# The seam between two expert layers: more PSUM banks and another order of products, and four of eight sums of x^T made earlier and kept in DRAM

## The chip, the core and the metric

One core of one Trainium2 chip runs the whole program. The metric is the device time of one execution in microseconds. The engines are named as in the profile: PE (TensorE's matrix products; PEld is its weight loads), DVE (VectorE), ACT (ScalarE), POOL (GpSimd) and SP (the queue that issues the DMAs).

## What is computed

A windowed attention feeds a first expert layer with a rational activation, and its result feeds a second one with an ELU activation. All data are float32.

```python
x = attention(q, k, v)              # 2304 tokens, 512 features
h = x @ w_in                        # layer 1: 512 -> 2048
P = a[0] + a[1]*h + a[2]*h**2 + a[3]*h**3
Q = 1.0 + abs(b[0])*abs(h) + abs(b[1])*h**2
x = (P / (Q + 1e-6)) @ w_out        # 2048 -> 512
h = x @ w2_in                       # layer 2: 512 -> 2048
g = where(h > 0, h, exp(min(h, 0)) - 1)
out = g @ w2_out                    # 2048 -> 512
```

## The kernel before, in words

Activations lie transposed, features on the partitions (`xT`). Every float32 operand of a product is split into a high part (rounded to fp32r by ACT) and a low part (the rest, a subtraction on DVE, line L864 in layer 2); a product is three passes on PE: high*high, low*high, high*low.

**Layer 1** goes over six blocks of 384 tokens and, in each, over 16 chunks of 128 hidden features: 96 steps `s`, with `f = s % 16`. In step `s` PE makes `gemm1(s)` (L251, 12 matmuls) and then `gemm2_T(s-3)` (L699, 12 matmuls), which takes the activation of three chunks earlier. `rational(s)` makes the activation. Its instructions stand in this order on the engines, and each engine works them off in that order. ACT: square L279, abs L280, two affine ones L281 and L284, then a logarithm L298 that needs DVE's `qq` of the same step, an exponential L299, and then what `after()` adds. DVE: L292 (high part of the chunk before), L295 (`qq` of this chunk), a slot `beside[1]`, L304, a slot `beside[2]`, L309, L312, L313. POOL makes the low part (L310).

**The last pass** (s = 80 to 95, the last block) also prepares layer 2. Layer 2 does its first product by a scheme with seven half-size products instead of eight (named b11, b21, t2, t3, t1, t4, b22), for which it needs four sums of x^T (two halves each: eight sums, L885, numbers n = 0 to 3) and four sums of the weights (`sum_w`, L837). The list `AT_ACT` says which high parts ACT copies at the end of which step, by `f`; the list `AT_DVE` holds the sums and the low parts, two of which the function `next_one` takes out per step, into the two slots of `rational`, from `f >= 3` on. A low part reads its high part.

**The seam** is the change from layer 1 to layer 2. Three `gemm2_T` (chunks 93 to 95, called G0, G1, G2 of pair 0) are left and are put between the products of pair 0. From there on layer 2 goes over pairs `q` of hidden chunks. Each pair has seven products (L907), added up on DVE from PSUM (L963: h11, u, v, h22, u2, h21, h12), four ELUs (ACT L969, L973, high part L995; DVE L978, low part L864), and four second products G0 to G3 (L923) of the pair before. The operands of pairs 1 and 2 (A to F) are prepared beside them. PE's order is written out by hand in `second(q)`; the order of the other engines comes from a planner, `in_order`, with estimated costs and due times. Two things in it are numbers: the time at which it takes ACT and DVE to be free.

PSUM has eight banks. At the seam banks 0 to 3 hold the accumulators of `gemm2_T`; 4, 5 and 7 the last three `h`; 6 the `qa` of `rational`. `m_first` says which bank each of the first seven products takes, after that banks 6 and 7 alternate. A product waits until the bank's last reader is done: the product b21 of pair 0, in bank 4, for L313 of step 94.

Of the kernel before, what the change touches and what calls it, by code (L numbers as in the profile page):

```python
# [44 lines left out]
def kernel(  # L45
# [13 lines left out]
    nc = tc.nc  # L59
# [627 lines left out]
    def experts():  # L687
# [182 lines left out]
        def sum_x(J, n, eng=nc.gpsimd, ks=range(2)):  # L870
# [9 lines left out]
            for k in ks:  # L880
# [3 lines left out]
                )[n]  # L884
                eng.tensor_tensor(out=sums[J, n][k], in0=x, in1=y, op=ALU.subtract)  # L885

        def hi_op(J, nm, k):
            if nm[0] == "t":
                src = sums[J, int(nm[1]) - 1][k]
            else:  # L890
                src = x_row(J, k + 2 * (nm[1] == "2"), nm[2] == "2")
            s = "_".join(map(str, x_slots[2 * ORDER.index(nm) + k]))
            XO[J, nm, k] = t = wpool.tile([P, 2, TB], F32R, tag=s, name=f"xo_{s}")
            nc.scalar.activation(out=t[:, 0], in_=src, func=AF.Copy)
            low_part[J, nm, k] = (t[:, 1], src, t[:, 0])

        m_banks = cycle((6, 7))
        m_first = [7, 4, 6, 7, 4, 6, 7]

        def product(q, nm):  # L900
            x, side = LIES[FACTOR[nm]]
# [110 lines left out]
        def second_product(q, n):  # L1012

            if q == 0:
                if n < 3:
                    step((q, "G", n), "PE", 2080, lambda: gemm2_T(NCH - 3 + n))
                return
            nm = ("h11", "h22", "h21", "h12")[n]
            x = "EF"[int(nm[1]) - 1]
            T = int(nm[2]) - 1  # L1020
            before = [((q - 1) // NP2 * NP2, "out", T, t) for t in range(NTT)]
            step((q, "G", n), "PE", 2080, lambda: gemm2(q - 1, nm), (q - 1, "lo", nm), (q - 1, "lo", x), *before)
# [52 lines left out]

        def second(q):
            p = q % NP2
            multiply(q, "b11", (q - 1, "h21"))
            multiply(q, "b21", (q - 1, "h12"))
            second_product(q, 0)  # L1080
            multiply(q, "t2", (q, "m1"))
            multiply(q, "t3", (q, "h11"))
            second_product(q, 1)
            multiply(q, "t1", (q, "u"))
            second_product(q, 2)
            multiply(q, "t4", (q, "v"))
            multiply(q, "b22", (q, "h22"), (q, "u2"))
            second_product(q, 3)
            step((q, "m1"), "ACT", 390, copy_of(q, "b11", "qq0"), (q, "b11"), (q - 1, "rest", "h22"))
            step((q, "h11"), "DVE", 480, added(q, "h11", "m1", "b21", "qq1"), (q, "m1"), (q, "b21"), (q - 1, "rest", "h11"))  # L1090
            elu_steps(q, "h11", "h11", "h2", [(q - 1, "lo", "h21")], [(q - 1, "G", 0)])
            step((q, "u"), "DVE", 480, added(q, "u", "m1", "t2", "ee0"), (q, "m1"), (q, "t2"), (q - 1, "rest", "h12"))
            step((q, "v"), "DVE", 480, added(q, "v", "u", "t3", "ee1"), (q, "u"), (q, "t3"), (q - 1, "rest", "h21"))
            step((q, "h22"), "DVE", 480, added(q, "h22", "v", "t1", "qq0"), (q, "v"), (q, "t1"))
            step((q, "u2"), "DVE", 480, added(q, "u", "u", "t1"), (q, "v"), (q, "t1"))
            elu_steps(q, "h22", "h22", "oo", [(q - 1, "lo", "h12")], [(q, "G", 1)])
            step((q, "h21"), "DVE", 480, added(q, "v", "v", "t4"), (q, "h22"), (q, "t4"))
            elu_steps(q, "h21", "v", "h2", [(q, "lo", "h11")], [(q - 1, "G", 2)])
            step((q, "h12"), "DVE", 480, added(q, "u", "u", "b22"), (q, "u2"), (q, "b22"))
            elu_steps(q, "h12", "u", "oo", [(q, "lo", "h22")], [(q - 1, "G", 3)])  # L1100
            weight_steps(q)
            if q == 0:
                x_steps(0, ("t4", "b22"), -1)
            if q > 0 and p == 0:
                for T in range(2):
                    for t in range(NTT):
                        step((q, "out", T, t), "ACT", 500, lambda T=T, t=t: put_out(q, T, t, "A"), (q, "G", 2 + T),
                             *[(q + 2 - 3, nm) for nm in ("b11", "b21", "t4", "t3", "b22")])
            if p == NP2 - 1 and q + 1 < NQ:
                x_sums(q // NP2 + 1, q)  # L1110
                x_steps(q // NP2 + 1, ORDER, q)

        def in_order():

            users, due, at_pe = {}, {}, 0
            for key, (_, _, _, needs) in todo.items():
                for n in needs:
                    users.setdefault(n, []).append(key)
            ideal = {}
            for key in pe_order:  # L1120
                ideal[key] = at_pe
                at_pe += todo[key][1]

            def begin(key):
                if key not in due:
                    engine, cost = todo[key][:2]
                    lag = cost + (3500 if engine == "SP" else 250)
                    t = min([begin(u) for u in users.get(key, [])], default=at_pe) - lag
                    due[key] = min(t, ideal.get(key, t))
                return due[key]  # L1130

            for key in todo:
                begin(key)
            free = {"PE": 0, "ACT": 3400, "DVE": 5500, "POOL": 0, "SP": 0}
            done, left, order, np = {}, dict(todo), [], 0
            missing = {key: sum(n in todo for n in set(needs)) for key, (_, _, _, needs) in todo.items()}
            ready = {key: 0 for key in todo if not missing[key]}
            while left:
                best = None
                for engine in free:  # L1140
                    cand = [(max(t, free[engine]), due[k], k) for k, t in ready.items() if todo[k][0] == engine]
                    if engine == "PE":
                        cand = [c for c in cand if c[2] == pe_order[np]]
                    if cand:
                        t0 = min(c[0] for c in cand)
                        c = min((c for c in cand if c[0] <= t0 + 60), key=lambda c: c[1])
                        if best is None or c[0] < best[0]:
                            best = c
                t, _, key = best
                engine, cost, fn, _ = todo[key]  # L1150
                free[engine] = t + cost
                end = t + cost + (3500 if engine == "SP" else 200)
                order.append((t, len(order), fn))
                del left[key], ready[key]
                np += engine == "PE"
                done[key] = end
                for u in users.get(key, []):
                    missing[u] -= 1
                    if not missing[u]:
                        ready[u] = max(done[n] for n in todo[u][3] if n in done)  # L1160
            return [fn for _, _, fn in sorted(order, key=lambda o: o[:2])]
# [10 lines left out]
        def x_hi(n, *ks):  # L1172
            return [lambda k=k: hi_op(0, ORDER[n], k) for k in ks]

        def w_hi(names):
            return [lambda x=x: hi_w(0, x) for x in names]

        AT_ACT = {6: x_hi(0, 0, 1), 9: w_hi("AB"), 10: x_hi(1, 0, 1), 11: w_hi("C") + x_hi(2, 0),
                  12: x_hi(2, 1) + w_hi("D"), 13: x_hi(3, 0, 1), 14: x_hi(4, 0, 1)}
        AT_DVE = [lambda n=n, k=k: sum_x(0, n, nc.vector, (k,)) for n in range(4) for k in range(2)]  # L1180
        AT_DVE += [lambda: lo((0, ORDER[0], 0)), lambda: lo((0, ORDER[0], 1))]
        AT_DVE += [lambda n=n: sum_w(0, nc.vector, (n,)) for n in range(4)]
        AT_DVE += [lambda key=key: lo(key) for key in (
            (0, "A"), (0, "B"), (0, ORDER[1], 0), (0, ORDER[1], 1), (0, "C"), (0, ORDER[2], 0),
            (0, ORDER[2], 1), (0, "D"), (0, ORDER[3], 0), (0, ORDER[3], 1), (0, ORDER[4], 0), (0, ORDER[4], 1),
        )]

        def prepare(s):
            f = s - LAST
            if f == 3:  # L1190
                load_wi(0)
            if f == 14:
                load_wi(1)
                for e in raw_ones(0):
                    load_raw(0, e)

            def copies():
                for fn in AT_ACT.get(f, []):
                    fn()

            def next_one():
                if f >= 3 and AT_DVE:
                    AT_DVE.pop(0)()
            rational(s, beside=(lambda: None, next_one, next_one), after=copies)

# [3 lines left out]

        SK = 3  # L1210
        nj = 0
        for s in range(NCH):
            o = s - SK
            j, f = divmod(s, KF)
# [10 lines left out]
                nj += 1  # L1225
            elif s >= LAST:
                prepare(s)
            else:
                rational(s, beside=(go_on, go_on, go_on))
            if s == KF - 2:  # L1230
# [45 lines left out]
```

## Time and profile before

| | |
|---|---|
| time, median of 3 runs | 932.92 us (931.76 to 934.11) |
| the profiled execution's own time | 933.09 us |
| its span, first to last instruction | 931.4 us |
| PE busy | 913.8 us, 98% |
| DVE busy | 792.0 us, 85% |
| ACT busy | 741.9 us, 80% |

Attention takes the first 150 us or so, the six passes of layer 1 go on to 540 us, layer 2 from there to the end. A profile's time column is counted from the first instruction. A row of the timeline gives the start, the duration, the engine, the line, what is written from what, and in brackets how long the engine had been idle before it and what released it. Durations reach to the acknowledged write; the next instruction on the same engine can start some 0.09 us before that.

### The profile page before, as it was taken

How to read it: one execution, taken by the hardware profiler on the slowest of the kernel's cores; microseconds unless marked ns; L12 is line 12 of the kernel's file. 1: busy time of each engine (PE TensorE's matmuls, PEld its weight loads, DVE VectorE, ACT ScalarE, POOL GpSimd, SP SyncE). 2: the span in 40 equal slices, each digit the busy share in tenths (PEclk: the TensorE clock that was granted, in tenths of full speed). 3: DMA queues.
4: the chain of work that ended last, by engine and by line, in shares of the span. 5: the costliest groups of instructions: out<-in, count | busy, mean ns of one | idle time of the engine just before them, and what ended most of it. 6: DMA issues, size and time to landing. Idle time of an engine off the chain costs nothing.

```text
span 931.4 us, 16710 instructions
## 1 busy us (share of the span) xinstructions
PE 913.8 (98%) x5494; PEld 838.8 (90%) x5494; DVE 792.0 (85%) x1863; ACT 741.9 (80%) x1623; POOL 185.2 (20%) x260
## 2 busy tenths in 40 slices
PE   8999999999999999999999989999999999999998
PEld 5777778999999999999999988898989898888887
DVE  7899998998998998988989999998968688677653
ACT  6999999889898898889888987666876567767553
POOL 5566661122222222222222210000000000000000
PEclk9999999999999999999999999999999999999999
DMA  9899951012222212222200133445243323442201
GB/s 195 217 242 230 236 154 67 1 35 68 86 68 79 89 56 92 85 63 86 86 30 29 38 110 113 158 157 171 91 162 110 115 81 100 147 147 80 80 0 68
DMA packets 112423, 98.35 MB, mean 106 GB/s; under 512 B 62800, under 2 KB 86096, under 8 KB 112336
## 3 DMA queue, kind: packets, MB, share of 16 engines
q1 hardware_dynamic: 109936, 96.70, 35.2%
q10 hardware_dynamic: 2400, 0.59, 0.4%
q8 instruction: 43, 0.70, 0.3%
q14 instruction: 44, 0.36, 0.1%
HBM read 79.96 MB, written 17.30 MB: 104 GB/s over the span
## 4 chain that ended last, share of the span: by engine, by line
PE 79%; DVE 14%; ACT 3%; DMA 2%; issue 1%; DVEq 0%; ACTq 0%; SPq 0%
PE acc L923 21%; PE m L907 18%; PE acc L699 18%; PE h L251 18%; DVE pr_wi L494 2%; DVE pr_wo L494 1%; DVE cvt L146 1%; PE s_ps L468 1%; DVE qkT L437 1%; DVE ghi L292 1%; PE x L561 1%; DVE ee L313 1%; DMA q_wo<-in_q_dram 1%; PE ps_pT L542 1%; DVE w_wi L160 1%
## 5 line engine op out<-in xcount | busy, mean ns | idle before, releaser
L251 PE MATMUL h<-xs,w_wi 128*128 128x384 f32 x1152 | 216.9, 335 | 0.0
L251 PEld LDWEIGHTS h<-xs,w_wi 128*128 128x128 f32 x1152 | 200.7, 188 | 1.2 <-DVE xs L227 0.6
L699 PE MATMUL acc<-ghi,w_wo 128*128 128x384 f32 x768 | 194.8, 334 | 0.0
L310 POOL TENSOR_TENSOR glo<-ee,rr 128x384 fp32r<-128x384 f32 x92 | 93.7, 1018 | 312.4 <-DVE ee L309 109.3
L699 PEld LDWEIGHTS acc<-ghi,w_wo 128*128 128x128 f32 x768 | 138.6, 188 | 0.0
L699 PE MATMUL acc<-glo,w_wo 128*128 128x384 f32 x384 | 128.4, 334 | 0.5 <-DVE glo L310 0.5
L923 PE MATMUL acc<-op_wo,ghi 128*128 128x512 f32 x288 | 90.0, 393 | 0.0
L907 PE MATMUL m<-xo_wo,op_wi 128*128 128x384 f32 x336 | 77.0, 337 | 2.3 <-DVE ee L963 2.3
L907 PE MATMUL m<-xo_wi,op_wi 128*128 128x384 f32 x336 | 78.0, 340 | 0.0
L969 ACT ACTIVATE oo<-qq 128x384 f32<-128x384 f32 x24 | 12.6, 526 | 77.0 <-DVE qq L963 77.0
L699 PEld LDWEIGHTS acc<-glo,w_wo 128*128 128x128 f32 x384 | 72.1, 188 | 0.8 <-DVE glo L310 0.8
L298 ACT ACTIVATE rr<-qq,c_q 128x384 f32<-128x384 f32 x96 | 59.2, 617 | 16.5 <-DVE qq L295 15.7
L281 ACT ACTIVATE oo<-h,a_sb 128x384 f32<-128x384 f32 x96 | 68.0, 708 | 3.3 <-DVE h L312 3.2
L284 ACT ACTIVATE ee<-h,a_sb 128x384 f32<-128x384 f32 x96 | 67.7, 705 | 0.0
L907 PEld LDWEIGHTS m<-xo_wo,op_wi 128*128 128x128 f32 x336 | 61.3, 189 | 6.4 <-ACT oo L973 2.5
L295 DVE SCALAR_TENSOR_TENSOR qq<-h,b_abs,qa 128x384 f32<-128x384 f32 x92 | 56.1, 610 | 12.4 <-ACT qa L280 11.3
L292 DVE TENSOR_TENSOR ghi<-ee,rr 128x384 fp32r<-128x384 f32 x96 | 53.5, 558 | 12.2 <-ACT h L279 0.5
L313 DVE TENSOR_TENSOR ee<-ee,h 128x384 f32<-128x384 f32 x96 | 53.3, 555 | 10.4 <-DVE h L312 0.5
L923 PEld LDWEIGHTS acc<-op_wo,ghi 128*128 128x128 f32 x288 | 53.8, 189 | 9.0
L907 PEld LDWEIGHTS m<-xo_wi,op_wi 128*128 128x128 f32 x336 | 61.1, 189 | 0.0
L279 ACT ACTIVATE h<-h 128x384 f32<-128x384 f32 x96 | 46.3, 483 | 14.8 <-PE h L251 14.2
L963 DVE TENSOR_TENSOR ee<-ee,m 128x384 f32<-128x384 f32 x96 | 52.8, 551 | 5.8 <-PE m L907 5.5
(192 smaller groups left out, 2068.4 us busy)
## 6 DMA issues: line engine op xcount, KB each, us to landing
pair<-joined_wo SPq DMA_DIRECT2D x43, 256.0 KB, 2.6
raw_wo<-in_moe_w_out_dram SPq DMA_DIRECT2D x20, 512.0 KB, 4.7
raw_wi<-in_moe_w_in_dram SPq DMA_DIRECT2D x16, 512.0 KB, 4.3
half<-in_moe_w_in_dram SPq DMA_DIRECT2D x32, 256.0 KB, 2.7
two_wo<-joined_wi SPq DMA_DIRECT2D x32, 256.0 KB, 2.8
s<-sums SPq DMA_DIRECT2D x32, 256.0 KB, 2.9
half<-in_moe_w_out_dram SPq DMA_DIRECT2D x22, 256.0 KB, 2.8
v<-in_v_dram SPq DMA_DIRECT2D x32, 128.0 KB, 3.3
```

What stands on the lines that cost most here:

```text
L251: nc.tensor.matmul(h, lhsT=WT["wi", f][:, SEL[wp], kk * P:(kk + 1) * P], rhs=x[xp][kk], start=(kk == 0 and n == 0), stop=(kk == KD - 1 and ...
L281: nc.scalar.activation(out=oo, in_=h2, func=AF.Identity, scale=a_sb[:, 3:4], bias=a_sb[:, 1:2])
L284: nc.scalar.activation(out=ee, in_=h2, func=AF.Identity, scale=a_sb[:, 2:3], bias=a_sb[:, 0:1])
L292: nc.vector.tensor_tensor(out=hi, in0=ee0, in1=rr0, op=ALU.mult)
L295: nc.vector.scalar_tensor_tensor(out=qq, in0=h2, scalar=b_abs[:, 1:2], in1=qa, op0=ALU.mult, op1=ALU.add)
L298: nc.scalar.activation(out=rr, in_=qq, func=AF.Ln, bias=c_q)
L310: (nc.gpsimd if c > 4 else nc.vector).tensor_tensor(out=low, in0=ee0, in1=rr0, op=ALU.mult)
L313: nc.vector.tensor_tensor(out=ee, in0=ee, in1=h, op=ALU.add)
L699: nc.tensor.matmul(acc_t[d], lhsT=WT["wo", f][:, SEL[wp], d * P:(d + 1) * P], rhs=gt[SEL[xp]], start=(f == 0 and n == 0), stop=(f == KF - ...
L907: nc.tensor.matmul(out, lhsT=w[:, SEL[wp], c0:c0 + P], rhs=XO[q // NP2, nm, k][:, SEL[xp]], start=(k == 0 and n == 0), stop=(k == 1 and n ...
L923: nc.tensor.matmul(acc_t[T, t], lhsT=gt[SEL[xp]][:, t * P:(t + 1) * P], rhs=w[:, SEL[wp]], start=(first and n == 0), stop=(last and n == 2),)
L963: nc.vector.tensor_tensor(out=t, in0=R[q, x], in1=M[q, m], op=ALU.add)
```

## The change

Three things are changed together.

1. Of the eight sums of x^T, the four with n = 0 and n = 2 are made in the middle passes, in steps 40, 48, 56 and 64, in which no other work takes the slots. Each is written to DRAM at once, and `load_sum` reads them back in steps 83 and 84. The four that are left are taken out from `f >= 4` on, and the two low parts of the product t4 stand at the end of the list; ACT's copies for t4 are added at f = 15.
2. The products of pair 0 take other banks, stand in another order among G0, G1 and G2, and wait for other things.
3. The planner takes ACT and DVE to be free 1200 and 1500 ns later.

```diff
+        EARLY = ((0, 0), (0, 1), (2, 0), (2, 1))
+        def store_sum(i):
+            n, k = EARLY[i]
+            b11, b12, b22 = [x_row(0, k + 2 * r, T) for r, T in ((0, 0), (0, 1), (1, 1))]
+            x, y = (b12, b11) if n == 0 else (b22, b12)
+            t = row("ghi3" if nj % 2 else "glo3")
+            nc.vector.tensor_tensor(out=t, in0=x, in1=y, op=ALU.subtract)
...
+            nc.sync.dma_start(out=stored[n][:, k * TB:(k + 1) * TB], in_=t)
+        def load_sum(n):
...
+            nc.sync.dma_start(out=t.rearrange("p k c -> p (k c)"), in_=stored[n])
-        m_first = [7, 4, 6, 7, 4, 6, 7]
+        m_first = [7, 4, 6, 5, 7, 4, 5]
...
-            multiply(q, "b11", (q - 1, "h21"))
-            multiply(q, "b21", (q - 1, "h12"))
+            multiply(q, "b11", (q - 1, "u" if q == 1 else "h21"))
+            multiply(q, "b21", *[(q - 1, n) for n in (("h22", "u2") if q == 1 else ("h12",))])
...
+            before = {"t2": "m1", "t3": "h11", "t1": "u", "t4": "v", "b22": "h22 u2"}
+            if q == 0:
+                before = {"t2": "", "t3": "", "t1": "m1", "t4": "h11", "b22": "v"}
...
-                x_steps(0, ("t4", "b22"), -1)
+                x_steps(0, ("b22",), -1)
...
-            free = {"PE": 0, "ACT": 3400, "DVE": 5500, "POOL": 0, "SP": 0}
+            free = {"PE": 0, "ACT": 4600, "DVE": 7000, "POOL": 0, "SP": 0}
...
-                  12: x_hi(2, 1) + w_hi("D"), 13: x_hi(3, 0, 1), 14: x_hi(4, 0, 1)}
-        AT_DVE = [lambda n=n, k=k: sum_x(0, n, nc.vector, (k,)) for n in range(4) for k in range(2)]
+                  12: x_hi(2, 1) + w_hi("D"), 13: x_hi(3, 0, 1), 14: x_hi(4, 0, 1), 15: x_hi(5, 0, 1)}
+        AT_DVE = [lambda n=n, k=k: sum_x(0, n, nc.vector, (k,)) for n in (1, 3) for k in range(2)]
...
+            (0, ORDER[5], 0), (0, ORDER[5], 1),
...
-                if f >= 3 and AT_DVE:
+                if f >= 4 and AT_DVE:
...
+        STORE_AT = [j * KF + f for j, f in ((2, 8), (3, 0), (3, 8), (4, 0))]
...
+            elif s in STORE_AT:
+                n = STORE_AT.index(s)
+                rational(s, beside=(lambda: None, lambda: store_sum(n), lambda: None))
```

How the instructions stand in the last pass. First ACT before, from the end of step 86: behind the exponential come the high parts of b11 (`xo_wo`, `xo_wi`), then step 87.

```order
L298 ACTIVATE rr_6847<-qq_6844,c_q 128x384
L299 ACTIVATE rr_6847<-rr_6847 128x384
L894 ACTIVATE xo_wo_6858<-xT 128x384
L894 ACTIVATE xo_wi_6860<-xT 128x384
L279 ACTIVATE h_6895<-h 128x384
```

DVE before, step 87 (its `qq` has the number 6897): the low parts of b11 stand in the two slots of this step, one step behind the copies on ACT.

```order
L292 TENSOR_TENSOR ghi_6905<-ee_6843,rr_6847 128x384
L295 SCALAR_TENSOR_TENSOR qq_6897<-h_6895,b_abs,qa 128x384
L864 TENSOR_TENSOR xo_wo_6858<-xT,xo_wo_6858 128x384
L304 SCALAR_TENSOR_TENSOR qq_6844<-qq_6844,ghi_6905 128x384
L864 TENSOR_TENSOR xo_wi_6860<-xT,xo_wi_6860 128x384
L309 TENSOR_TENSOR ee_6843<-ee_6843,qq_6844 128x384
```

ACT in the change, step 86 (`qq_6859`):

```order
L298 ACTIVATE rr_6862<-qq_6859,c_q 128x384
L299 ACTIVATE rr_6862<-rr_6862 128x384
L914 ACTIVATE xo_wo_6873<-xT 128x384
L914 ACTIVATE xo_wi_6875<-xT 128x384
L279 ACTIVATE h_6909<-h 128x384
```

DVE in the change, step 86 as well: the list is shorter by the four sums and starts one step later, so that the low parts of b11 now stand right behind the `qq_6859` that ACT's L298 reads, in the same step as their copies. The same goes for all the low parts behind them in the list.

```order
L292 TENSOR_TENSOR ghi_6867<-ee_6809,rr_6813 128x384
L295 SCALAR_TENSOR_TENSOR qq_6859<-h_6857,b_abs,qa 128x384
L864 TENSOR_TENSOR xo_wo_6873<-xT,xo_wo_6873 128x384
L304 SCALAR_TENSOR_TENSOR qq_6810<-qq_6810,ghi_6867 128x384
L864 TENSOR_TENSOR xo_wi_6875<-xT,xo_wi_6875 128x384
L309 TENSOR_TENSOR ee_6809<-ee_6809,qq_6810 128x384
```

The seam on ACT before: the high part of pair 0's h11 (`ghi_7449`), then the four copies of x^T out of the accumulators of G2, then a weight's high part.

```order
L859 ACTIVATE op_wi_7432<-two_wo_7370 128x256
L995 ACTIVATE ghi_7449<-h_7406 128x384
L705 ACTIVATE xT<-acc 128x384 x4
L859 ACTIVATE op_wi_7473<-s_7444 128x512
L969 ACTIVATE oo<-qq_7471 128x384
```

The same place in the change: the high part of h11 (`ghi_7483`) stands behind the four copies.

```order
L859 ACTIVATE op_wi_7454<-two_wo_7388 128x256
L705 ACTIVATE xT<-acc 128x384 x4
L1015 ACTIVATE ghi_7483<-h_7445 128x384
L989 ACTIVATE oo<-qq_7481 128x384
L993 ACTIVATE oo<-oo,c_m 128x384
```

The seam on DVE before, from the `h11` of pair 1 (`qq_7547`) to its `u` (`ee_7580`), which frees the bank that its product t1 takes:

```order
L963 TENSOR_TENSOR qq_7547<-qq_7527,m 128x384
L864 TENSOR_TENSOR op_wi_7426<-pair,op_wi_7426 128x512
L978 SCALAR_TENSOR_TENSOR h_7505<-h_7505,ee_7424 128x384
L864 TENSOR_TENSOR op_wi_7429<-two_wo_7370,op_wi_7429 128x512
L978 SCALAR_TENSOR_TENSOR oo<-oo,ee_7396 128x384
L864 TENSOR_TENSOR glo_7559<-h_7505,ghi_7558 128x384
L963 TENSOR_TENSOR ee_7580<-qq_7527,m 128x384
```

In the change, from two rows behind that h11 to the same `u` (`ee_7612`): h21, then two low parts of weights, and pair 2's four sums of weights stand ahead of it.

```order
L983 TENSOR_TENSOR ee_7450<-ee_7450,m 128x384
L864 TENSOR_TENSOR op_wi_7426<-pair,op_wi_7426 128x512
L864 TENSOR_TENSOR op_wi_7448<-two_wo_7388,op_wi_7448 128x512
L837 TENSOR_TENSOR s_7581<-two_wo_7388 128x256
L837 TENSOR_TENSOR s_7581<-s_7581,two_wo_7388 128x256
L837 TENSOR_TENSOR s_7582<-two_wo_7388 128x256
L837 TENSOR_TENSOR s_7582<-two_wo_7388,s_7581 128x256
L998 SCALAR_TENSOR_TENSOR oo<-oo,ee_7440 128x384
L998 SCALAR_TENSOR_TENSOR h_7568<-h_7568,ee_7450 128x384
L983 TENSOR_TENSOR ee_7612<-qq_7535,m 128x384
```

On PE, the product t1 of pair 0 moves from behind G1 to ahead of it, and t4 from behind G2 to ahead of it; nothing else moves there.

## Rows read from the trace of the kernel before

**Rows 1.** Busy time by stretch, all engines; then granted clock, DMA share, GB/s.

```profile
400.00:500.00 100.00, 100.00 (x579) 100.00 (x578) 88.08 (x186) 88.12 (x174) 24.28 (x24) 1.00 0.20 64
500.00:600.00 100.00, 97.49 (x519) 92.67 (x518) 95.12 (x197) 79.31 (x157) 12.21 (x12) 0.98 0.27 87
```

**Rows 2.** Timeline of PE at the seam, from 540 us on.

```profile
540.01 0.68 PE L907 MATMUL m<-xo_wo,op_wo 128*128 128x384 f32 x3
...
541.46 0.80 PE L907 MATMUL m<-xo_wo,op_wo 128*128 128x384 f32 x3 [0.25 <-DVE ee L313]
...
556.49 0.77 PE L907 MATMUL m<-xo_wo,op_wi 128*128 128x384 f32 x3 [2.26 <-DVE ee L963]
...
567.54 0.63 PE L923 MATMUL acc<-op_wi,ghi 128*128 128x512 f32 x2
```

**Rows 3.** PE by stretch: length, busy (instructions), granted clock, DMA share, GB/s.

```profile
559.00:560.00 1.00, 1.00 (x5) 0.50 0.00 0
```

**Rows 4.** The chain that ended last: start, length, engine, line, matmuls.

```profile
556.49 3.50 PE m L907 x12
...
569.78 2.10 PE m L907 x12
```

**Rows 5.** All waits of DVE, 483 to 550 us: total, times, longest.

```profile
DVE qq L295 <- ACT qa L280: 2.6, 1, 2.6
DVE ee L313 <- DVE h L312: 0.5, 1, 0.5
```

**Rows 6.** Timeline of DVE, step 94 and the start of step 95.

```profile
537.79 0.61 DVE L295 SCALAR_TENSOR_TENSOR qq<-h,b_abs,qa 128x384 f32<-128x384 f32 x1
538.31 0.56 DVE L864 TENSOR_TENSOR xo_wo<-t_wo,xo_wo 128x384 fp32r<-128x384 f32 x1
538.78 0.55 DVE L304 SCALAR_TENSOR_TENSOR qq<-qq,ghi 128x384 f32<-128x384 f32 x1
...
542.01 0.61 DVE L295 SCALAR_TENSOR_TENSOR qq<-h,b_abs,qa 128x384 f32<-128x384 f32 x1
```

**Rows 7.** Timeline of DVE, step 40 from L292 to the next L292.

```profile
310.83 0.56 DVE L292 TENSOR_TENSOR ghi<-ee,rr 128x384 fp32r<-128x384 f32 x1
...
314.24 0.56 DVE L292 TENSOR_TENSOR ghi<-ee,rr 128x384 fp32r<-128x384 f32 x1
```

**Rows 8.** Timeline of ACT, a 512-wide copy, then step 94.

```profile
526.57 0.62 ACT L859 ACTIVATE op_wi<-s 128x512 fp32r<-128x512 f32 x1
...
538.43 0.62 ACT L298 ACTIVATE rr<-qq,c_q 128x384 f32<-128x384 f32 x1 [0.31 <-DVE qq L295]
539.08 0.53 ACT L299 ACTIVATE rr<-rr 128x384 f32<-128x384 f32 x1
539.51 0.51 ACT L894 ACTIVATE xo_wo<-t_wi 128x384 fp32r<-128x384 f32 x1
```

**Rows 9.** Timeline of DVE, step 82.

```profile
487.48 0.61 DVE L295 SCALAR_TENSOR_TENSOR qq<-h,b_abs,qa 128x384 f32<-128x384 f32 x1 [2.58 <-ACT qa L280]
488.01 0.42 DVE L772 SCALAR_TENSOR_TENSOR glo<-glo,half 128x256 int32<-128x256 int32 x1
```

**Rows 10.** Timeline of DVE at the seam.

```profile
547.64 0.56 DVE L963 TENSOR_TENSOR qq<-qq,m 128x384 f32<-128x384 f32 x1
...
551.98 0.42 DVE L837 TENSOR_TENSOR s<-two_wo 128x256 f32<-128x256 f32 x1
...
553.45 0.55 DVE L963 TENSOR_TENSOR qq<-ee,m 128x384 f32<-128x384 f32 x1
...
557.18 0.70 DVE L864 TENSOR_TENSOR op_wo<-s,op_wo 128x512 fp32r<-128x512 f32 x1
557.78 0.69 DVE L864 TENSOR_TENSOR op_wi<-s,op_wi 128x512 fp32r<-128x512 f32 x1
...
560.09 0.55 DVE L963 TENSOR_TENSOR qq<-qq,m 128x384 f32<-128x384 f32 x1 [1.15 <-PE m L907]
...
563.55 0.55 DVE L963 TENSOR_TENSOR ee<-qq,m 128x384 f32<-128x384 f32 x1 [0.29 <-PE m L907]
```

More of the change, by code (lines that the diff above doesn't have):

```diff
@@ L885, in sum_x @@
                 eng.tensor_tensor(out=sums[J, n][k], in0=x, in1=y, op=ALU.subtract)
+        EARLY = ((0, 0), (0, 1), (2, 0), (2, 1))
+        stored = {}
+        def store_sum(i):
[4 more added lines that the diff above has]
+            nc.vector.tensor_tensor(out=t, in0=x, in1=y, op=ALU.subtract)
+            if k == 0:
+                stored[n] = dram.tile([P, 2 * TB], F32, name=f"x_sum_{n}")
+            nc.sync.dma_start(out=stored[n][:, k * TB:(k + 1) * TB], in_=t)
+        def load_sum(n):
+            nm = "_".join(map(str, t_slots[n]))
+            t = wpool.tile([P, 2, TB], F32, tag=nm, name=f"t_{nm}")
+            sums[0, n] = [t[:, k] for k in range(2)]
+            nc.sync.dma_start(out=t.rearrange("p k c -> p (k c)"), in_=stored[n])
         def hi_op(J, nm, k):
@@ L1014, in second_product @@
             if q == 0:
-                if n < 3:
-                    step((q, "G", n), "PE", 2080, lambda: gemm2_T(NCH - 3 + n))
+                step((q, "G", n), "PE", 2080, lambda: gemm2_T(NCH - 3 + n))
                 return
@@ L1077, in second, with next_product @@
             p = q % NP2
-            multiply(q, "b11", (q - 1, "h21"))
-            multiply(q, "b21", (q - 1, "h12"))
+            multiply(q, "b11", (q - 1, "u" if q == 1 else "h21"))
+            multiply(q, "b21", *[(q - 1, n) for n in (("h22", "u2") if q == 1 else ("h12",))])
             second_product(q, 0)
[L1081 to L1088, printed above, removed]
+            before = {"t2": "m1", "t3": "h11", "t1": "u", "t4": "v", "b22": "h22 u2"}
+            if q == 0:
+                before = {"t2": "", "t3": "", "t1": "m1", "t4": "h11", "b22": "v"}
+            def next_product(nm):
+                multiply(q, nm, *[(q, n) for n in before[nm].split()])
+            next_product("t2")
+            next_product("t3")
+            if q:
+                second_product(q, 1)
+            next_product("t1")
+            second_product(q, 2 if q else 1)
+            next_product("t4")
+            if q == 0:
+                second_product(q, 2)
+            next_product("b22")
+            if q:
+                second_product(q, 3)
             step((q, "m1"), "ACT", 390, copy_of(q, "b11", "qq0"), (q, "b11"), (q - 1, "rest", "h22"))
@@ L1190, in prepare @@
             if f == 3:
+                load_sum(0)
                 load_wi(0)
+            if f == 4:
+                load_sum(2)
             if f == 14:
```

## The prediction, made before the change was run

> **What bounds the kernel now.** I read the busy times by stretch first, then PE's own timeline at the seam, then DVE's waits and timeline around it. In 400 to 500 us PE is busy all the time, and DVE and ACT 88 us each; in 500 to 600 us PE still is 97.49 us, but DVE has risen to 95.12 [rows 1]. So PE bounds layer 1, and in the last pass DVE, which then makes sums and low parts beside the activation, comes close behind it. The reader should see two things at the seam [rows 2]. The product b21 of pair 0 waits 0.25 us at 541.46 for L313, the end of a step of the activation: by then PE has no lead over DVE left, and whatever DVE loses more before this point, PE loses as well. And b11 of pair 1 waits 2.26 us at 556.49 for DVE's h21. These two are the 2.5 us that PE misses in 500 to 600 us. After the second the granted clock is 0.50, the lower level of 1.2 GHz [rows 3], and the product of twelve matmuls takes 3.50 us where another takes 2.10 [rows 4]: 1.4 us, and some 0.4 in the first matmuls of the next product, as an estimate from the same ratio; 1.8 us for one fall of the clock. The most that any repair of this seam can give is therefore 2.5 + 1.8 = 4.3 us, or 0.5%.
>
> From 483 to 550 us DVE waits twice [rows 5], 2.58 us for ACT's `qa` in step 82 and 0.45 for its own result. After that it goes from one instruction to the next: a step with both slots filled takes 537.79 to 542.01, 4.22 us [rows 6], while PE's two products take 2 x 2.10 = 4.20 [rows 4]. A wait that is put into a DVE step of the last pass therefore has no cover.
>
> I follow the change to one point, the first matmul of G2 of pair 1 (L923, at 567.54 [rows 2]): from there PE is busy to the end, so the shift of this point is the shift of the time.
>
> **The middle passes.** Four subtractions of 0.47 us each (issue to issue, 538.31 to 538.78 [rows 6]) go into steps 40 to 64. A step without work in the slots takes DVE 310.83 to 314.24, 3.41 us [rows 7]; with one more, 3.88, less than PE's 4.20. PE hides it. If DVE had no slack there, it would be 1.9 us in all; PE's 100.00 of 100 and DVE's 88.08 at 400 to 500 us [rows 1] speak for slack. Six more DMAs on SP cost nothing: DMA engines are 20% busy [rows 1], and the sums read back in steps 83 and 84 are first read as operands several steps of 4 us later. I take 0 for this part.
>
> **The last pass, what is saved.** Four sums go, two low parts (of t4) come. The list starts one step later, so step 83 loses both fillings: 4.22 - 3.41 = 0.81 us less for DVE.
>
> **The last pass, what is added.** Four entries fewer at the front and a start one step later (two entries) bring each low part one step nearer to ACT's copies: into the step whose `after()` makes the copy it reads. Before, b11's low part stood in step 87 behind a copy of step 86; now it stands in step 86, directly behind that step's L295. But the copy stands on ACT behind L298 and L299, and L298 reads what this same L295 writes. So DVE, with L304, L309, L312 and L313 queued behind the low part, has to sit out a round trip. Worked out from step 94: L295 takes 0.61 us from its start and 0.03 more to ACT's start (537.79 to 538.43); L298 to L299 0.65; L299 to the copy 0.43; the copy 0.51; 0.03 back to DVE as on the way out, an estimate [rows 6, 8]. That is 2.26 us from the start of L295 to that of the low part, against 0.52 today [rows 6]: a wait of 1.74. Where a copy 512 wide comes first, it is 0.62 instead of 0.51 [rows 8], so 1.85. The second slot's copy comes 0.43 after the first, while DVE's second slot comes 0.94 after it: no second wait.
>
> The steps concerned are f = 6 (b11), 9 (A, B), 10 (b21), 11 (C, t2), 12 (t2, D), 13 (t3), 14 (t1), 15 (t4): eight, two of them (9 and 11) with the wide copy. 6 x 1.74 + 2 x 1.85 = 14.14 us; less the 0.81, DVE comes to the seam 13.33 us later. The h11 of pair 0 moves from 547.64 [rows 10] to 560.97. The step of the pass becomes 4.22 + 1.74 = 5.96 us, PE's 4.20 has gaps of some 1.8 in it.
>
> The bounds of one wait: below, 0 if ACT made the copies ahead of L298, which the order excludes; above 2.58, what DVE has waited for ACT in one step [rows 9]. The terms that I add are all rows of one step, so I take 1.74, and 0.2 less or more for how a start overlaps the end before it.
>
> **The rule of order, weighed.** In step 82 L295 waited 2.58 us for ACT, and L772 behind it, which does not read what ACT made, started only at 488.01, after it [rows 9]: DVE kept its order. On that the sum rests: nothing behind a waiting low part moves ahead of it. The Trainium skill, "Perfetto Trace Analysis", section "Per-instruction lifecycle: what the profiler-reported window actually captures", says the same in a few words: TensorE can pull weight loads ahead, while VectorE, ScalarE and GpSimd are strictly first in, first out. By that rule the time is the sum below; were VectorE free to pass, the last rival's time would stand.
>
> **The seam.** From pair 0's h11 to the u of pair 1, which now frees the bank of t1 of pair 1, DVE has in the new order 16 instructions of 384 at 0.47 us [rows 6], 6 of 512 at 0.60 (557.18 to 557.78), one of 256 at 0.37 and two sets of four weight sums at 1.47 (551.98 to 553.45) [rows 10]: 7.52 + 3.60 + 0.37 + 2.94 = 14.43 us. Between the same points it has 1.15 + 0.29 = 1.44 us of waits now [rows 10]; with the h11's high part behind the four x^T copies on ACT I take 1.3, with bounds of 0 and 1.44 or somewhat more. So 15.7: u at 560.97 + 15.7 = 576.67, 0.55 for it, 0.12 to PE as an estimate of the hand-off, and t1 takes 1.05 (half of 2.10 [rows 4]): G2 of pair 1 at 578.4, 10.86 us later than 567.54. The banks themselves do what they are for: on time, h11 at 547.64 would give u at 563.3 and G2 at 565.1, 2.5 us earlier than now, and with the 0.81 also 564.3. That is 2.5 to 3.3 us of gain against 14.1 of new waits.
>
> **The sum.** 933.09 of the profiled execution + 10.86 = 943.95, so 944.0 us; the median is 0.17 lower than that execution, which I leave out.
>
> **The rivals.** *The clock falls as well.* PE gets gaps of 1.8 us in each of eight steps. What a lower clock costs inside the pass lies in the gaps, but between PE's wait for t3 and G2 of pair 0, and after the wait for t1 of pair 1, nothing covers it: one or two falls of 1.8 us [rows 4] give 945.8 to 947.6, slightly more if the clock stays down in the pass too. For it speaks the 0.50 after 2.26 us of wait [rows 3]; against it that each gap here is shorter and PE works between them. *The waits are smaller.* If ACT ran ahead so that each wait were about 1 us, DVE would lose 8 - 0.81 = 7.2 in place of 13.3: 938. Against it: L298 itself waited 0.31 us for L295 in step 94 [rows 8], so ACT has no more to give away. *The other side: the low parts do not hold DVE.* If they found their copies made, or later instructions filled the wait, the seam's gain would stand, 933.09 - 3.3 = 929.8, faster by 0.35%. It decides at the point where the eight waits come to 3.3 us in all, 0.41 each.
>
> **How the numbers follow.** The forecast 944.0 has a chance of 0.72, the falls of the clock 0.13, the smaller waits 0.10, the other side 0.05. The forecast's own range is 941 (each wait 0.2 shorter: 1.6; no waits in the seam: 1.3) to 946. With the rival of the clock the range is 941 to 948; it leaves out the smaller waits, the other side and a little beyond. A measurement of this kernel tells 0.3%, 2.8 us, from no change. Slower has all of the first three cases, except waits that nearly cancel against the gain, 0.03, which go to no change; the last case is 929.8 at its best and smaller with any rest of a wait, so it is split: faster 0.04, same 0.04, slower 0.92.
>
> **What would show it.** In the changed profile DVE's waits should list a low part (L864) waiting for ACT's copy (L914) eight times, 1.5 to 2 us each, some 14 in all, and L292 to L292 in those steps should be near 5.96 us. PE should wait in the second half of the pass, some 1.8 us a step, and its busy time at 500 to 550 us should fall by over a quarter. h11 of pair 0 should come near 561, u of pair 1 near 576.7, and behind G2 of pair 1 near 578.4 nothing should differ. Step 40 should stay at 4.2 us with no wait of PE. I am wrong if those L864 start half a microsecond after L295, if PE is not held by them, or if the time between h11 and u of pair 1 differs from 15.7 by more than 2 us.

## The result and the profile after

| | before | changed |
|---|---|---|
| median | 932.34 us (931.30 to 934.11, 4 runs) | 944.32 us (943.32 to 945.48, 4 runs) |
| ratio to before | | 1.0127 [1.0114, 1.0140] |
| profiled execution, span | 933.09, 931.4 us | 944.07, 942.4 us |

The changed kernel is slower by 12 us, and the forecast was 944.0. First, DVE's waits of the changed kernel from 483 to 580 us: what waits and for whom; total, times and longest in us. They answer to [rows 5].

```profile
DVE xo_wo L864 <- ACT xo_wo L914: 8.3, 5, 1.7
DVE qq L295 <- ACT qa L280: 2.6, 1, 2.6
DVE op_wi L864 <- ACT op_wi L859: 2.5, 2, 1.8
DVE op_wo L864 <- ACT op_wo L859: 1.8, 1, 1.8
DVE xo_wi L864 <- ACT xo_wi L914: 1.7, 1, 1.7
DVE glo L864 <- ACT ghi L1015: 0.2, 1, 0.2
DVE oo L998 <- ACT oo L993: 0.2, 1, 0.2
```

The reader should see a low part (L864) waiting for its own copy on ACT (L914 and L859) in four of the first five rows, nine waits in all. Eight of them are in the last pass; the ninth, 0.79 us of the 2.5, is in the seam, as are the two of the last rows. What one looks like, DVE's timeline of step 94 shows, as [rows 6] does for before:

```profile
547.15 0.56 DVE L292 TENSOR_TENSOR ghi<-ee,rr 128x384 fp32r<-128x384 f32 x1
547.63 0.61 DVE L295 SCALAR_TENSOR_TENSOR qq<-h,b_abs,qa 128x384 f32<-128x384 f32 x1
549.89 0.56 DVE L864 TENSOR_TENSOR xo_wo<-t_wi,xo_wo 128x384 fp32r<-128x384 f32 x1 [1.66 <-ACT xo_wo L914]
550.37 0.55 DVE L304 SCALAR_TENSOR_TENSOR qq<-qq,ghi 128x384 f32<-128x384 f32 x1
...
553.09 0.56 DVE L292 TENSOR_TENSOR ghi<-ee,rr 128x384 fp32r<-128x384 f32 x1
```

and ACT's timeline of the same 2.3 us, which shows what DVE waited for:

```profile
548.27 0.62 ACT L298 ACTIVATE rr<-qq,c_q 128x384 f32<-128x384 f32 x1 [0.45 <-DVE qq L295]
548.92 0.53 ACT L299 ACTIVATE rr<-rr 128x384 f32<-128x384 f32 x1
549.35 0.51 ACT L914 ACTIVATE xo_wo<-t_wi 128x384 fp32r<-128x384 f32 x1
```

Read the two together: ACT waits for DVE's L295, and DVE then waits for ACT's copy, which stands two instructions behind. From L295 to the low part it is 2.26 us, as worked out, against 0.52 in [rows 6]: 1.74 us lost. (The bracket says 1.66, because the profile counts the wait from the recorded end of L295, and without a wait the low part starts some 0.09 us before that end.) From L292 to L292 the step takes 5.94 us. PE feels it. Its waits from 483 to 600 us:

```profile
PE acc L699 <- POOL glo L310: 7.0, 5, 1.7
PE m L927 <- ACT oo L281: 3.0, 1, 3.0
PE m L927 <- DVE ee L983: 1.3, 1, 1.3
```

The first row is the gap in five steps of the pass: `gemm2_T` waits for POOL's low part, which follows DVE. The first such gap, 0.72 us, ends only at 523.01, after the second of DVE's waits, because PE had low parts in stock until then: POOL finished one at 503.04 that PE took at 505.49, 2.45 us later; after the first of DVE's waits 0.64 us of this was left, two steps without a wait brought it back to 1.08, and the second wait used it up. The second row is b21 of pair 0, the third t1 of pair 1. For b21 the profile names ACT's L281, which ended at 553.13; by the kernel L281 does not touch the bank, and L313 of step 94, which frees it, ended at 552.98. Those two on PE's own timeline, with the first matmul of G2 of pair 1 behind (as [rows 2]):

```profile
553.13 0.76 PE L927 MATMUL m<-xo_wo,op_wo 128*128 128x384 f32 x3 [2.95 <-ACT oo L281]
...
577.26 0.81 PE L927 MATMUL m<-xo_wo,op_wo 128*128 128x384 f32 x3 [1.28 <-DVE ee L983]
...
578.44 0.63 PE L943 MATMUL acc<-op_wi,ghi 128*128 128x512 f32 x2
```

And DVE's h11 of pair 0 and u of pair 1, which answer to the first and last row of [rows 10]:

```profile
560.90 0.55 DVE L983 TENSOR_TENSOR qq<-qq,m 128x384 f32<-128x384 f32 x1
...
576.66 0.55 DVE L983 TENSOR_TENSOR ee<-qq,m 128x384 f32<-128x384 f32 x1
```

Behind G2 of pair 1 there are 942.4 - 578.44 = 363.96 us left, and 931.4 - 567.54 = 363.86 before [rows 2]: nothing there has changed by more than 0.1 us.

### The profile page after: what moved, and what is told of

It is laid out like the page before. It is cut to its first block, busy times and chain, and to the rows that moved or that the text cites. A ratio compares the mean times of both kernels' runs of the same rounds, so it can differ in the third digit from the quotient of the medians.

```text
span 942.4 us, 16713 instructions
## 1 busy us (share of the span) xinstructions
PE 915.2 (97%) x5494; PEld 838.7 (89%) x5494; DVE 792.1 (84%) x1863; ACT 742.8 (79%) x1623; POOL 184.1 (20%) x260
## 4 chain that ended last, share of the span: by engine, by line
PE 80%; DVE 12%; ACT 4%; DMA 2%; issue 1%; SPq 1%; ACTq 0%; DVEq 0%
PE acc L943 21%; PE acc L699 19%; PE m L927 18%; PE h L251 18%; DMA q_wo<-in_q_dram 1%; DVE pr_wi L494 1%; DVE pr_wo L494 1%; PE s_ps L468 1%; DVE cvt L146 1%; PE x L561 1%; PE ps_pT L542 1%; DVE qkT L437 1%; PE ps_qk L412 1%; ACT rr L298 1%; DVE w_wi L160 1%
## 5 line engine op out<-in xcount | busy, mean ns | idle before, releaser
L281 ACT ACTIVATE oo<-h,a_sb 128x384 f32<-128x384 f32 x96 | 68.0, 708 | 11.9 <-DVE h L312 11.7
L298 ACT ACTIVATE rr<-qq,c_q 128x384 f32<-128x384 f32 x96 | 59.1, 616 | 18.9 <-DVE qq L295 18.2
L295 DVE SCALAR_TENSOR_TENSOR qq<-h,b_abs,qa 128x384 f32<-128x384 f32 x92 | 56.0, 609 | 11.3 <-ACT qa L280 10.5
L292 DVE TENSOR_TENSOR ghi<-ee,rr 128x384 fp32r<-128x384 f32 x96 | 53.5, 557 | 11.6
L313 DVE TENSOR_TENSOR ee<-ee,h 128x384 f32<-128x384 f32 x96 | 53.3, 555 | 10.0
```

The lines of the kernel that those rows point to most:

```text
L281: nc.scalar.activation(out=oo, in_=h2, func=AF.Identity, scale=a_sb[:, 3:4], bias=a_sb[:, 1:2])
L292: nc.vector.tensor_tensor(out=hi, in0=ee0, in1=rr0, op=ALU.mult)
L295: nc.vector.scalar_tensor_tensor(out=qq, in0=h2, scalar=b_abs[:, 1:2], in1=qa, op0=ALU.mult, op1=ALU.add)
L298: nc.scalar.activation(out=rr, in_=qq, func=AF.Ln, bias=c_q)
L313: nc.vector.tensor_tensor(out=ee, in0=ee, in1=h, op=ALU.add)
```

## The experiments

In all runs the column "G2" below is the first matmul of G2 of pair 1. One thing must be taken off when traces are compared: an execution reaches layer 1 earlier or later than another, by up to 1.2 us here, before any changed instruction. The `qq` of step 82, which waits for ACT in every run, marks it: 487.48 before [rows 9], 487.98 in the changed kernel, 487.24 to 488.67 in the experiments. The mark lies behind the steps that make the four early sums, but they don't move it: from the first row of step 40 [rows 7] to it there are 176.65 us before, 176.67 in the changed kernel and 176.65 or 176.66 in the experiments. The shifts below are against this mark.

| run | median us | ratio to before | waits in the pass | shift of h11 of pair 0 | shift of G2 |
|---|---|---|---|---|---|
| changed | 944.32 | 1.0127 | 8 | +12.76 | +10.40 |
| low parts one step later | 930.19 | 0.9971 [0.9960, 0.9983] | 0 | -1.63 | -3.19 |
| copies ahead of L298 | 931.11 | 0.9980 [0.9969, 0.9990] | 8 of 0.1 to 0.2 | 0.00 | -2.43 |
| before, copies later | 944.23 | 1.0121 [1.0105, 1.0136] | 7 | +12.22 | +10.65 |
| five waits | 937.72 | 1.0052 [1.0038, 1.0066] | 5 | +6.92 | +4.52 |
| seam only | 930.40 | 0.9971 [0.9960, 0.9983] | 0 | 0.00 | -2.40 |
| sums only | 930.31 | 0.9972 [0.9961, 0.9982] | 0 | -1.63 | -3.19 |
| low parts later, u first | 929.24 | 0.9961 [0.9947, 0.9974] | 0 | -1.63 | -4.36 |

**Low parts one step later.** The changed kernel, with all else as it is:

```diff
+                for k in range(2):
+                    step(("xlo", 0, "t4", k), "DVE", 470, lambda k=k: lo((0, "t4", k)))
                 x_steps(0, ("b22",), -1)
...
-            (0, ORDER[5], 0), (0, ORDER[5], 1),
...
-                if f >= 4 and AT_DVE:
+                if f >= 5 and AT_DVE:
```

> The changed kernel, with the list of DVE started one step later again (f >= 5), so that each low part stands one step behind its copy, and the two low parts of t4 taken in the seam. Theory (the twelve microseconds are the eight waits of a low part for a copy behind L298): no wait of L864 for L914 or L859 in the pass; DVE has two steps without slots, 1.62 us less than before, and reaches h11 of pair 0 near 546; u of pair 1 near 562.7, G2 of pair 1 near 564.4, so 3.1 us better than before: 929 to 930.5. Rival (the new order and banks of the seam, or the planner's later start, cost the time): nothing of that is undone, 942 to 944. Rival (the sums in DRAM cost something): between 932 and 935.

It came to 930.19 us: the 14 us between this and the changed kernel hang on where sixteen low parts stand (with the sums of the same list). DVE's waits from 483 to 570 us in this run:

```profile
DVE qq L295 <- ACT qa L280: 2.6, 1, 2.6
DVE ee L313 <- ACT h L279: 0.5, 1, 0.5
DVE oo L998 <- ACT oo L993: 0.4, 1, 0.4
DVE op_wi L864 <- ACT op_wi L859: 0.3, 1, 0.3
```

No wait for a copy is left in the pass; the last row lies in the seam. Both rivals fall with it: seam and sums in DRAM are all still in this kernel, and it is faster than before. PE has one wait left, which the last experiment takes up:

```profile
564.01 0.81 PE L927 MATMUL m<-xo_wo,op_wo 128*128 128x384 f32 x3 [1.13 <-DVE ee L983]
```

**Copies ahead of L298.** The low parts stay in the step of their copies; only ACT's order changes:

```diff
+            after()
             nc.scalar.activation(out=rr, in_=qq, func=AF.Ln, bias=c_q)
             nc.scalar.activation(out=rr, in_=rr, func=AF.Exp, scale=-1.0)
             q_t[c] = (qq, ee, rr)
-        after()
```

> The changed kernel with its low parts where they are, in the step of their copies, but with ACT's copies put ahead of L298 instead of behind L299. Theory (DVE waits because the copy stands behind an instruction that reads what the same step's L295 writes): the copy then needs nothing of L295; it ends about 0.2 to 0.3 us after the low part could start, eight times, 2 us in all; of the seam's 3.3 us a gain of about 1.3 to 1.7 is left: 931 to 932. Rival (ACT has too much work in the pass, and the copies come late for that): L298 is now later by two copies, and DVE waits for ACT elsewhere, 940 to 944.

931.11 us. Step 94 on ACT (L299 is the logarithm here, a line lower) and on DVE:

```profile
537.12 0.71 ACT L284 ACTIVATE ee<-h,a_sb 128x384 f32<-128x384 f32 x1
537.73 0.51 ACT L914 ACTIVATE xo_wo<-t_wi 128x384 fp32r<-128x384 f32 x1
538.15 0.51 ACT L914 ACTIVATE xo_wi<-t_wi 128x384 fp32r<-128x384 f32 x1
538.56 0.60 ACT L299 ACTIVATE rr<-qq,c_q 128x384 f32<-128x384 f32 x1
...
537.64 0.61 DVE L295 SCALAR_TENSOR_TENSOR qq<-h,b_abs,qa 128x384 f32<-128x384 f32 x1
538.27 0.56 DVE L864 TENSOR_TENSOR xo_wo<-t_wi,xo_wo 128x384 fp32r<-128x384 f32 x1
```

The low part starts 0.63 us after L295, 0.11 later than with no dependence in the way (0.52), and not 2.26; in the eight steps it is 0.11 six times and 0.22 twice, where a wide copy comes first (0.2 to 0.3 expected), so little that the profile lists no wait of a low part in this pass. So it is not the amount of work on ACT, and not that both stand in one step: it is that the copy stands behind an instruction which needs the L295 of that step.

**Before, copies later.** The kernel before, and nothing but this:

```diff
-        AT_ACT = {6: x_hi(0, 0, 1), 9: w_hi("AB"), 10: x_hi(1, 0, 1), 11: w_hi("C") + x_hi(2, 0),
-                  12: x_hi(2, 1) + w_hi("D"), 13: x_hi(3, 0, 1), 14: x_hi(4, 0, 1)}
+        AT_ACT = {7: x_hi(0, 0, 1), 10: w_hi("AB"), 11: x_hi(1, 0, 1), 12: w_hi("C") + x_hi(2, 0),
+                  13: x_hi(2, 1) + w_hi("D"), 14: x_hi(3, 0, 1), 15: x_hi(4, 0, 1)}
```

> The kernel before with only this changed: ACT makes each group of high parts one step later (7, 10 to 15 in place of 6, 9 to 14), so that seven low parts come to stand in the step of their copies. Banks, order, sums and planner are those of before. Theory: seven waits, two of them with the wide copy, 12.4 us on DVE, less the 0.45 of its own wait; all of it reaches the end: 944 to 945.5. Rival (the waits hide behind PE, and the time of the change comes from the seam): 932 to 934.

944.23 us: seven waits put into the kernel before, without banks, order or sums of the change, make it as slow as the change. DVE came 12.22 us later to h11 (expected 12.4 less 0.45, 11.95, but its own 0.45 us wait was still there); G2 shifted only 10.65. The rest is the clock behind b11 of pair 1, of which the last section tells.

**Five waits.** The changed kernel with two empty entries ahead of the low parts of t3; t4's low parts go to the seam as in the first experiment:

```diff
-        AT_DVE += [lambda key=key: lo(key) for key in (
+        AT_DVE += [lambda key=key: key and lo(key) for key in (
...
-            (0, ORDER[2], 1), (0, "D"), (0, ORDER[3], 0), (0, ORDER[3], 1), (0, ORDER[4], 0), (0, ORDER[4], 1),
-            (0, ORDER[5], 0), (0, ORDER[5], 1),
+            (0, ORDER[2], 1), (0, "D"), None, None, (0, ORDER[3], 0), (0, ORDER[3], 1), (0, ORDER[4], 0), (0, ORDER[4], 1),
```

> The changed kernel with two empty entries put into DVE's list ahead of the low parts of t3, so that those of t3 and t1 stand one step behind their copies, and those of t4 in the seam: five waits in place of eight. Theory (each wait costs its 1.74 us in full, by a straight line): 8.9 us of waits, less 1.62 for two steps without slots and 0.45, plus 0.94 for t4's low parts in the seam: G2 of pair 1 near 572.9, 938.4 us, bounds 937 to 940. Rival (only the waits at the end of the pass reach the seam, since the earlier ones are caught up): the last three gone, 930 to 933. Rival (the first ones alone break the pipeline): 942 to 944.

937.72 us, between the two. Against the run with none, DVE reaches h11 8.55 us later, five waits of 1.74 to 1.85 being 8.92, less the 0.46 us that L313 waits in the run with none and not in this one. Neither the first nor the last waits alone make the loss. G2 shifts by 7.71 of these 8.55, mainly since DVE no longer waits for ACT in the seam, which it did for 0.36 and 0.27 us in the run with none.

**Seam only.** The second and third part of the change put into the kernel before, whose last pass stays:

```diff
-        m_first = [7, 4, 6, 7, 4, 6, 7]
+        m_first = [7, 4, 6, 5, 7, 4, 5]
...
-            free = {"PE": 0, "ACT": 3400, "DVE": 5500, "POOL": 0, "SP": 0}
+            free = {"PE": 0, "ACT": 4600, "DVE": 7000, "POOL": 0, "SP": 0}
```

(with the whole order of `second(q)` of the change between them).

> The kernel before with the second and third part of the change alone: banks, order, what products wait for, and the planner's two numbers are those of the change; the last pass (eight sums, low parts one step behind their copies) is that of before, and t4's parts are made in the seam. Theory (the seam by itself is a small gain): h11 of pair 0 stays at 547.6; to u of pair 1 it is 16.6 us as in the run with the later low parts, so u near 564.2, G2 of pair 1 near 565.9 in place of 567.5: 1.6 us better, about 931 (930.3 to 932). Rival (the new seam costs part of the 11 us): 934 or more.

930.40 us: the seam alone is a gain, 2.40 us at G2. That is more than the 1.6 expected, because from h11 to u it took 15.73 us and not 16.6: DVE did not wait for ACT here. b11 of pair 1 no longer waits for h21, and no clock falls behind it; what PE waits for now is u, for 1.32 us:

```profile
563.73 0.81 PE L907 MATMUL m<-xo_wo,op_wo 128*128 128x384 f32 x3 [1.32 <-DVE ee L963]
```

**Sums only.** The first part of the change put into the kernel before, with the low parts a step behind their copies:

```diff
-                if f >= 3 and AT_DVE:
+                if f >= 5 and AT_DVE:
...
+            elif s in STORE_AT:
+                n = STORE_AT.index(s)
+                rational(s, beside=(lambda: None, lambda: store_sum(n), lambda: None))
```

> The kernel before with the first part alone: four sums in the middle passes, written out and read back, and the list of DVE started at f >= 5, so that the low parts stay one step behind their copies; banks, order and planner are those of before, and t4's parts are made in the seam. Theory (the sums by themselves cost nothing and take two steps' slots, 1.6 us, from a DVE that limits the seam): h21 of pair 0 comes 1.6 to 2 us earlier, the wait of b11 of pair 1 shrinks from 2.26 to near 0.5 and the clock does not fall behind it: 1.6 to 3.4 us better, about 930 (929 to 931.3). Rival (writing and reading them in DRAM costs PE time in the middle passes): 932.5 or more.

930.31 us. b11 of pair 1 still waits for h21, but half as long, and its clock stays at 1.00. The wait is longer than the 0.5 us expected: h21 came 1.6 us earlier, but PE, which no longer waits at b21 of pair 0, got there 0.5 earlier too:

```profile
555.75 0.76 PE L927 MATMUL m<-xo_wo,op_wi 128*128 128x384 f32 x3 [1.16 <-DVE ee L983]
```

Each part of the change is worth about 2.5 us, the two together hardly more (930.19): both end or shorten the same wait of PE in the seam, and both keep the clock from falling behind it, which is about 1 us of the 2.5 (the last section has the numbers). Where both are made, u on DVE is next.

**Low parts later, u first.** The first experiment, and in the planner one more need for the sums of weights of pair 2:

```diff
-                    step((w, "sum"), "DVE", 1400, lambda: sum_w(w, eng), (w, "load"), *gone, (w - 1, "kept"))
+                    step((w, "sum"), "DVE", 1400, lambda: sum_w(w, eng), (w, "load"), *gone, (w - 1, "kept"), *([(1, "u")] if w == 2 else []))
```

> The kernel with the later low parts and, in addition, the sums of weights of pair 2 held back behind u of pair 1. Theory (what is left in the seam is t1 of pair 1 waiting 1.13 us for u, which stands behind these four sums, 1.47 us): the wait goes, and nothing else comes late: 1.1 us better than the later low parts alone, about 929. Rival (the operands C and D of pair 2 come late instead): 930 to 932.

929.24 us, faster than both kernels: 3.6 us or 0.39% under before, 15 under the changed one. G2 comes 1.17 us earlier than in the first experiment, whose one wait was 1.13. Busy time by stretch, engines in the order PE, PEld, DVE, ACT, POOL, then clock:

```profile
480.00:540.00 60.00, 60.00 (x348) 60.00 (x347) 53.60 (x109) 54.19 (x106) 14.43 (x15) 1.00 0.16 53
540.00:570.00 30.00, 30.00 (x161) 28.09 (x160) 28.71 (x60) 23.62 (x50) 2.10 (x3) 1.00 0.36 115
```

PE has no gap left from layer 1 into layer 2.

## Why the prediction was right, step by step

- **The middle passes, 0.** Right. Step 40 of the changed kernel on DVE, with the new subtraction (L896), takes 311.31 to 315.19, the 3.88 us worked out:

```profile
311.31 0.56 DVE L292 TENSOR_TENSOR ghi<-ee,rr 128x384 fp32r<-128x384 f32 x1
311.79 0.61 DVE L295 SCALAR_TENSOR_TENSOR qq<-h,b_abs,qa 128x384 f32<-128x384 f32 x1
312.32 0.55 DVE L896 TENSOR_TENSOR glo<-xT 128x384 f32<-128x384 f32 x1
...
315.19 0.56 DVE L292 TENSOR_TENSOR ghi<-ee,rr 128x384 fp32r<-128x384 f32 x1
```

  The run with the sums alone, faster than before, shows the same for the DRAM traffic, and so do the 176.65 and 176.67 us from step 40 to the mark.
- **The last pass, eight waits.** Right in place, number and size: 2.26 us from L295 to the low part. DVE came 12.76 us later to h11, not 13.33. Of these 0.57 us, 0.45 are the wait of L313 for its own product [rows 5], which did not come again; the sum had left it in. The steps with a wait are 1.72 us longer than those of before [rows 6], not 1.74; over eight waits this makes about the rest.
- **The order of the queue.** As the rule of the Trainium skill weighed in the prediction ("Perfetto Trace Analysis", "Per-instruction lifecycle: what the profiler-reported window actually captures") has it, DVE kept its order: L304 reads what L292 of the same step and L295 of the step before have written, and stood behind the waiting low part all the same; in the trace above it starts at 550.37, behind the low part of 549.89.
- **The seam, 15.7 us from h11 to u.** Measured 560.90 to 576.66, 15.76, of which 1.13 are waits for ACT (1.3 assumed).
- **PE's gaps.** Their size was nearly right (1.47 to 1.72 us, and 1.8 forecast), their number was not: PE's busy time from 500 to 550 us fell to 42.97 of 50, 14% and not the quarter that was forecast. The row below has PE's busy time behind the length, the clock third from the end:

```profile
500.00:550.00 50.00, 42.97 (x241) 41.23 (x239) 36.23 (x73) 36.85 (x70) 9.06 (x9) 1.00 0.13 43
```

  "A wait that is put into a DVE step of the last pass therefore has no cover" is so for DVE, and for PE only from the third wait on: the first fell into PE's stock of 2.45 us altogether, the second in part, and f = 7 and 8 have none. The time gains nothing by that, since at the end of the pass DVE sets the seam, whatever PE did before.
- **The sum, +10.86.** Measured against the mark of step 82: +10.40. The 0.46 too much are the 0.57 of the last pass, less 0.1 for the way from h11 to G2. That the time came within 0.32 us of the forecast owes a little to chance: the profiled execution was 0.5 us late before the first changed instruction, which made up for it.
- **The rival of the clock** happened, and cost nothing that can be seen. Against it the prediction had said that each gap would be shorter than the 2.26 us of [rows 2]; this was wrong for b21 of pair 0. After its wait of 2.95 us PE ran at a granted clock of 0.50, the lower level of 1.2 GHz, until 557:

```profile
553.00:555.00 2.00, 1.87 (x8) 0.74 0.00 0
555.00:557.00 2.00, 2.00 (x8) 0.50 0.00 0
557.00:559.00 2.00, 2.00 (x11) 0.91 0.01 4
```

  The prediction had found nothing that covers a fall between PE's wait for t3 and G2 of pair 0; this one came a little earlier, and it is covered: DVE goes on without waiting for PE, sets u of pair 1 at 576.66, and PE waits 1.28 us for it there. From h11 to u it is 15.76 us here and 15.72 in the run with the copies ahead, which has the same seam and PE at 1.00 all through it. The price of a fall, 1.8 us, was too high as well: it compares 3.50 with 2.10 us, and the product behind such a wait takes 2.32 without a fall (last section).
- **The other side.** The kernel without waits is 930.19, the rival's 929.8: the gain of the seam that the prediction set against the waits is there.

## What to carry to other kernels

In queues that keep their order, an instruction of one engine that reads what another makes should stand behind it by one full step of the loop, or the source must stand ahead of whatever the second engine takes from the first in that step; otherwise two engines that are 85 and 80% busy wait for each other in every step. When entries are taken out of a list that fills slots, the entries behind them move up, and each has to be held against its source again: here four subtractions less and a start one step later cost 12 us, and `f >= 5` in place of `f >= 4` (with two low parts moved to the seam) gives 14 back. Two repairs of the same wait don't add up; after each, look at what is late next.

## What the runs showed of the hardware that was not expected

The same wait at the same place can lower the clock or leave it high. b11 of pair 1 waits 2.26 us before [rows 2], the granted clock falls to 0.50 [rows 3], and its twelve matmuls take 3.50 us [rows 4]. In the run of the kernel before with later copies it waits 2.28 us for the same DVE instruction, behind the same products, and the clock stays (it had been at 0.50 once already, at 555 to 557 us, behind a wait of 2.95 us at b21 of pair 0); windows of PE (length, busy, granted clock, DMA share, GB/s) and the product in the chain:

```profile
569.00:571.00 2.00, 1.11 (x6) 1.00 0.47 131
571.00:573.00 2.00, 2.00 (x12) 1.00 0.00 0
...
569.89 2.32 PE m L907 x12
```

The product takes 2.32 us there and 3.50 with the fall, 1.2 us more; with the slower start of the next product the fall costs 1.55 us in all, which is nearly all of the 1.57 by which G2 in that run shifted less than h11.

Even one and the same kernel does both. Of the 30 executions of the kernel before that were run beside the experiments, 10 have a mean granted clock of 1.000, with a median of 931.9 us, and 20 one of 0.998 or less, with a median of 933.2. The 1.3 us between them are near the price of one fall; where in an execution the clock fell is seen only in the one profiled, which is of the second kind. So about 1 us of the gain of the two partial runs is the clock: against the executions of before with 1.000 alone, the run with the seam only gains 931.9 - 930.4 = 1.5 us, and not 2.5.

In the changed kernel the gaps of 0.7 to 1.7 us in five steps of the pass left the clock at 1.00, and the wait of 2.95 lowered it, as it did in the kernel with later copies. What decides it at a wait of 2.26 or 2.28 us, these runs don't settle.
